# New tile order, split statistics and a rewritten instruction order at the start of the first MLP

## Chip, cores and metric

One core of a Trainium2 chip runs the whole chain. The metric is the time of one execution on the device in microseconds. The engines are TensorE (PE in the profile, its weight loads PEld), VectorE (DVE), ScalarE (ACT), GpSimd (POOL), and SyncE (SP), which starts most DMAs.

## The reference

Three layers follow one another; the output of each is the input of the next. B=4, H=8, S=768, D=40, so a batch is 768 tokens by 320 values: six tiles of 128 tokens, 24 tiles in all.

```python
# 1: linear attention over 768 steps, state 40x40 for each head
y[t] = r[t] @ state
Sa = state @ a[t]
state = state * w[t] - outer(Sa, b[t]) + outer(v[t], k[t])
# 2: Fourier mixing, then a channel MLP (320 -> 1280 -> 320)
u = x + real(fft(fft(x, axis=1), axis=2))
un = (u - mean(u)) / sqrt(var(u) + 1e-6)      # over the 320 channels of a token
x = u + relu(un @ w_ch1) @ w_ch2
# 3: token MLP (768 -> 256 -> 768), then a channel MLP (320 -> 1536 -> 320)
u = x + (relu(x.T @ w_tok1) @ w_tok2).T
out = u + relu(u @ w_ch1) @ w_ch2
```

## The kernel before

**Order.** Every instruction is first recorded by `Plan.op` with its engine and the buffers that it reads and writes. Nothing is scheduled by a rule: the string `ORDER` lists the numbers of the recorded operations in base 36, and `Plan.emit` issues them in that order. Each engine works through its own instructions in this order. A number followed by `:0` or `:1` names the PSUM banks that the operation takes, and `+12,y,0` puts twelve filler matmuls (`warm`, L54, on the identity) into a bank of the pool y.

**Attention.** Class `Attn` takes the sequence in 12 chunks of 64 steps; a small triangular inverse on VectorE, products on TensorE and selections on GpSimd follow each other in every chunk. Its result is X, the 24 tiles in SBUF; a batch's last tiles are written by the line X<-y (L434).

**Fourier mixing, batch by batch.** `fft` forms sums and differences of halves of X on VectorE (FP and FM L876, ef L877 and L878, sd L882, dd L888), splits each into a rounded part Xh and a rest Xl (L884, L885; Ds L889, L890), and multiplies with the transform tables in PSUM (psA, L900 and L915). The results are evacuated as a rounded part (ScalarE, L925) and a rest (VectorE, L926) into A. `fft2` then runs four mixing groups of eight matmuls "mix" (L947). Each is added to X while the sum over the channels is accumulated in sm (VectorE, L950), and a Square with accumulation gives ss (ScalarE, L953). Group 0 completes the tiles 0 and 3, group 1 the tiles 1 and 4, group 2 tile 2 and 96 rows of tile 5, and group 3 the other 32 rows of 5. After all six tiles one set of small instructions on 6 columns forms the variance v (L960), its square root y (ScalarE, L961), the reciprocal (L962), a Newton step (L963 to L966, four instructions) and the bias nb (L967).

**First channel MLP.** The tokens go through in six groups of four tiles, `tiles(g)`: tiles 0 to 3 of batch 0, then 4 and 5 of batch 0 with 0 and 1 of batch 1, and so on. `norm` applies y and nb (Y, L976 on VectorE, L978 on ScalarE), `turnp` transposes Y on TensorE (trp L1018) and evacuates it as cc, and `ch` multiplies: hps L1047, then acc L1037. The mixing of the next batch and the transposes of the next group are recorded within a group's `ch`.

**Token MLP and last MLP.** `tok` gives tps (L1179), `tok2` t2ps (L1192), which is added to X by X<-t2ps (L1194). `turnd` transposes the four tiles of a group with VectorE (L986, L987), stores and loads them again (dr_T, Z) and forms sums on GpSimd; `ch7` multiplies (sa and sb L1084, acc L1073).

**Decoding of weights.** Beside all this the weights, which lie in 64-bit numbers, are decoded in pieces: mdraw is loaded, mdt and mda are formed on VectorE (L853, L854, L856, L857), mdh on ScalarE (L855), and GpSimd finishes mda (L858, L859).

## Time and profile before

| | us |
|---|---|
| median of 3 runs | 979.46 |
| lowest and highest | 975.63, 984.27 |
| the profiled execution | 969.72 |
| its span, first to last instruction | 968.0 |
| TensorE busy | 914.7 (94%) |
| VectorE busy | 702.4 (73%) |
| ScalarE busy | 491.8 (51%) |
| GpSimd busy | 367.6 (38%) |
| warm fillers on TensorE, within its busy time | 74.2 |

The span is the time between the first and the last instruction of the profiled execution; its own time has 1.7 us more around it. Busy TensorE includes the fillers and the time in which a matmul runs at a low clock. The granted clock of the span was 0.974 of full speed. In the profile every fp32 matmul of the program is two records.

### The profile page before, as it was taken

Reading aid. Unit: us, or ns where it says so; the run is one execution under the profiler, and the core shown is the slowest. Engines: PE = TensorE matmul, PEld = TensorE weight load, DVE = VectorE, ACT = ScalarE, POOL = GpSimd, SP = SyncE. Lnnn points to the kernel's source line nnn. Section 1 sums busy time; section 2 is a strip of 40 time slices with the busy share of each in tenths; the row PEclk is TensorE's granted clock in tenths of the full one; section 3 lists DMA queues with packets and bytes.
Section 4 is the critical chain, followed back from the end, with each engine's and each line's share of the span. In section 5 each row is a group of like instructions: output and inputs, shape, how many; then the busy total and the mean of one; then the engine's idle time right before and its main releaser. Section 6 shows DMA issues by size and latency. Waiting matters only on the chain.

```text
span 968.0 us, 24200 instructions
## 1 busy us (share of the span) xinstructions
PE 914.7 (94%) x9657; PEld 848.1 (88%) x9657; DVE 702.4 (73%) x1527; ACT 491.8 (51%) x1068; POOL 367.6 (38%) x498
## 2 busy tenths in 40 slices
...
GB/s 213 155 169 174 174 196 215 180 199 203 170 183 171 180 242 286 287 140 194 126 172 123 151 86 109 132 166 374 144 175 86 80 50 79 101 1 99 1 28 28
...
## 3 DMA queue, kind: packets, MB, share of 16 engines
...
## 4 chain that ended last, share of the span: by engine, by line
PE 71%; DVE 9%; DMA 5%; ACT 3%; issue 2%; POOL 2%; SPq 1%; DVEq 0%; POOLq 0%; ACTq 0%
PE acc L1073 13%; PE hps L1047 9%; PE acc L1037 8%; PE sb L1084 7%; PE sa L1084 5%; PE sc L406 4%; PE kg L216 3%; PE warm L54 3%; PE tps L1179 2%; PE t2ps L1192 2%; PE y L428 1%; PE x L343 1%; PE s L367 1%; PE mix L947 1%; PE mg L291 1%
## 5 line engine op out<-in xcount | busy, mean ns | idle before, releaser
L1047 PE MATMUL hps<-cc,W1t 128*128 128x512 f32 x480 | 120.7, 395 | 0.0
L1037 PE MATMUL acc<-W,cc 128*128 128x320 f32 x720 | 116.1, 310 | 0.3 <-DMA W<-m11l 0.3
L1037 PEld LDWEIGHTS acc<-W,cc 128*128 128x128 f32 x720 | 109.0, 188 | 4.8 <-DMA W<-m11l 0.7
L1047 PEld LDWEIGHTS hps<-cc,W1t 128*128 128x128 f32 x480 | 87.9, 188 | 16.4
L1097 POOL TENSOR_TENSOR C<-C,C 128x256 f32<-128x256 f32 x36 | 27.4, 760 | 173.0 <-DVE W1t L1090 115.3
L1049 ACT ACTIVATE cc<-hps 128x512 fp32r<-128x512 f32 x60 | 35.8, 597 | 100.2 <-PE hps L1047 100.2
L1050 DVE SCALAR_TENSOR_TENSOR cc<-hps,cc 128x512 fp32r<-128x512 f32 x60 | 41.3, 688 | 56.6 <-ACT cc L1049 56.4
L54 PE MATMUL warm<-ident 128*128 128x128 f32 x454 | 74.2, 301 | 2.9 <-POOL ident masks.py:199 2.0
L216 PE MATMUL kg<-am,bt 120*128 120x192 f32 x242 | 55.7, 366 | 18.0 <-ACT am L136 15.7
L416 POOL TENSOR_SCALAR_AFFINE_SELECT sc<-sc 64x384 f32<-64x384 f32 (+1 forms) x72 | 42.3, 588 | 80.1 <-ACT sc L136 71.5
L225 POOL TENSOR_SCALAR_AFFINE_SELECT RT<-RT 64x384 f32<-64x384 f32 (+1 forms) x66 | 42.2, 659 | 78.4 <-ACT RT L136 77.2
L1091 DVE TENSOR_TENSOR C<-sb,C 128x256 f32<-128x256 f32 x108 | 44.2, 421 | 33.3 <-PE sb L1084 26.9
L54 PEld LDWEIGHTS warm<-ident 128*128 128x128 f32 x454 | 63.6, 207 | 5.2 <-POOL ident masks.py:199 2.0
L1073 PE MATMUL acc<-v,W1t 128*128 128x320 f32 x432 | 67.2, 309 | 0.0
L1073 PE MATMUL acc<-vb,W1t 128*128 128x320 f32 x432 | 66.9, 309 | 0.0
L1089 ACT ACTIVATE W1t<-C 128x256 fp32r<-128x256 f32 x108 | 41.9, 413 | 45.5 <-DVE C L1091 36.6
L1073 PEld LDWEIGHTS acc<-v,W1t 128*128 128x128 f32 x432 | 63.7, 188 | 0.1
L1073 PEld LDWEIGHTS acc<-vb,W1t 128*128 128x128 f32 x432 | 63.7, 188 | 0.0
L216 PEld LDWEIGHTS kg<-am,bt 120*128 120x128 f32 x242 | 43.0, 209 | 21.8 <-ACT am L136 16.8
L1090 DVE SCALAR_TENSOR_TENSOR W1t<-C,W1t 128x256 fp32r<-128x256 f32 x108 | 46.6, 450 | 19.4 <-ACT W1t L1089 19.0
L406 PE MATMUL sc<-rm,VZd 120*128 120x192 f32 x264 | 59.4, 358 | 0.3 <-ACT RT L136 0.3
L858 POOL TENSOR_TENSOR mda<-mda,mdh 128x320 f32<-128x320 f32 (+2 forms) x32 | 29.6, 933 | 72.2 <-ACT mdh L855 54.0
...
## 6 DMA issues: line engine op xcount, KB each, us to landing
...
mdraw<-in_moe_w_ch_dram SPq DMA_DIRECT2D x22, 320.0 KB
...
```

The lines of the kernel that those rows point to most:

```text
L54: for x in range(m): nc.tensor.matmul(t[:,128*(x%4):128*(x%4)+128],lhsT=ident,rhs=ident,start=True,stop=True)
L216: nc.tensor.matmul(ps[:,192*x:192*x+192],lhsT=bt[:,g+x].rearrange("p v t -> p (v t)"),rhs=am[:,:,g+x],start=True,stop=True)
L225: nc.gpsimd.affine_select(out=kv,in_=kv,pattern=[[0,3*m],[1,L]],compare_op=ALU.is_gt,fill=0.0,base=0,channel_multiplier=-1)
L406: for x,g in enumerate(gs): nc.tensor.matmul(ps[:,192*x:192*x+192],lhsT=VZd[:,g].rearrange("p v t -> p (v t)"),rhs=s.rm[:,:,g],start=True, ...
L416: nc.gpsimd.affine_select(out=o,in_=o,pattern=[[0,3*m],[-1 if rv else 1,L]],compare_op=ALU.is_gt,fill=0.0,base=L-1 if rv else 0,channel_mu ...
L1037: nc.tensor.matmul(s.pst(acc[x]),lhsT=a[:,sl],rhs=w2(w,m),start=(m==0 and n==0),stop=(m==MT-1 and n==2))
L1047: for n,(l,r) in enumerate(ops): nc.tensor.matmul(ps,lhsT=l,rhs=r,start=n==0,stop=n==7)
L1073: nc.tensor.matmul(s.pst(acc[x]),lhsT=a[:,sl],rhs=wv(w),start=(u==0 and y==0 and k==0),stop=(u==5 and y==1 and k==2))
L1084: for n,(y,x) in enumerate(((0,0),(0,1),(1,0),(2,2))): nc.tensor.matmul(R[r](),lhsT=va(q,y),rhs=S[:,x],start=first and n==0,stop=last and ...
L1089: s.act(256,lambda: nc.scalar.activation(out=Hh(y,c),in_=src(),func=AF.Relu),rd,[('Hh',z,y,c)],free=free)
L1090: s.dve(.33,lambda: V.scalar_tensor_tensor(out=Hl(y,c),in0=src(),scalar=0.0,in1=Hh(y,c).bitcast(F32),op0=ALU.max,op1=ALU.subtract),rd+[('H ...
L1091: def add(n,r,m,free): s.dve(.33,lambda: V.tensor_tensor(out=C(n),in0=R[r](),in1=C(m),op=ALU.add),[K[r],('C',m)],[('C',n)],free=free)
```

## The change

`TI=(0,3,1,4,2,5)` is a new order of a batch's six tiles. `tiles(g)` uses it, so that the first group takes the tiles 0, 3, 1 and 4 of batch 0, and the statistics sm, ss, v, y and nb hold their columns in this order. For batch 0 the root and its refinement are recorded in two sets, on the columns 0 to 3 and 4 to 5; for the other batches in one. The Newton step has three instructions in place of four: q=y*v, q=(q*-0.5)*y, y=(q+1.5)*y. `init` sets one value sq1 and takes its square root on ScalarE, which loads the table of the root there. The string `ORDER` is another one throughout. The lines of the new kernel stand one lower up to L953 and three or four lower behind it (v is L964, the reciprocal L966, Y L979 and L981, hps L1050).

```diff
+TI=(0,3,1,4,2,5)
...
     def init(s):
+        s.one(s.sq1,['sq1']); s.P.op('ACT',.1,lambda: s.nc.scalar.activation(out=s.sq1,in_=s.sq1,func=AF.Sqrt),[],['sq1'])
         s.zero(s.D1,['D1'],.63); s.one(s.D1[:,:,0:1],['D1'])
...
 ORDER="""
-0 1 5 4 2 fg 7 8 6 e 3 9 1b f g h +12,y,0 bx:0 1d 1f 1e a br 3s 1c 3u 8n 3v 3y 3w 7i 3t 7k 3x 3z j bk:1 by bz:0 bl i o m n k bm:1 bn b c d +3,y,0 s:0
...
-        Y=lambda: t["y"][b%2]; NB_=lambda: t["nb"][b%2]
-        s.dve(.07,lambda: V.tensor_scalar(out=t["v"],in0=t["ss"],scalar1=320.0**-3,scalar2=1e-6,op0=ALU.mult,op1=ALU.add),[('ss',i) for i in range(6)],['lv'])
-        s.act(54,lambda: nc.scalar.activation(out=Y(),in_=t["v"],func=AF.Sqrt),['lv'],[('ly',b%2)])
-        s.dve(.1,lambda: V.reciprocal(out=Y(),in_=Y()),[],[('ly',b%2)])
-        s.dve(.07,lambda: V.tensor_tensor(out=t["q"],in0=Y(),in1=Y(),op=ALU.mult),[('ly',b%2)],['lq'])
-        s.dve(.07,lambda: V.tensor_tensor(out=t["q"],in0=t["q"],in1=t["v"],op=ALU.mult),['lv'],['lq'])
-        s.dve(.07,lambda: V.tensor_scalar(out=t["q"],in0=t["q"],scalar1=-0.5,scalar2=1.5,op0=ALU.mult,op1=ALU.add),[],['lq'])
-        s.dve(.07,lambda: V.tensor_tensor(out=Y(),in0=Y(),in1=t["q"],op=ALU.mult),['lq'],[('ly',b%2)])
...
-    def tiles(s,g): return [divmod(4*g+x,6) for x in range(4)]
+        for c0,c1 in ((0,4),(4,6)) if b==0 else ((0,6),):
+            Y=lambda c0=c0,c1=c1: t["y"][b%2][:,c0:c1]; g=lambda n,c0=c0,c1=c1: t[n][:,c0:c1]; qs=TI[c0:c1]; z=c0//4
...
+            s.dve(.07,lambda g=g: V.tensor_scalar(out=g("v"),in0=g("ss"),scalar1=320.0**-3,scalar2=1e-6,op0=ALU.mult,op1=ALU.add),[('ss',i) for i in qs],kv)
+            s.act(54,lambda g=g,Y=Y: nc.scalar.activation(out=Y(),in_=g("v"),func=AF.Sqrt),kv,ky)
+            s.dve(.1,lambda Y=Y: V.reciprocal(out=Y(),in_=Y()),[],ky)
+            s.dve(.07,lambda g=g,Y=Y: V.tensor_tensor(out=g("q"),in0=Y(),in1=g("v"),op=ALU.mult),ky+kv,kq)
+            s.dve(.07,lambda g=g,Y=Y: V.scalar_tensor_tensor(out=g("q"),in0=g("q"),scalar=-0.5,in1=Y(),op0=ALU.mult,op1=ALU.mult),ky,kq)
+            s.dve(.07,lambda g=g,Y=Y: V.scalar_tensor_tensor(out=Y(),in0=g("q"),scalar=1.5,in1=Y(),op0=ALU.add,op1=ALU.mult),kq,ky)
...
+    def tiles(s,g): return [((4*g+x)//6,TI[(4*g+x)%6]) for x in range(4)]
```

What the new `ORDER` moves is seen in the engines' queues, at three places. The first is VectorE between the last X<-y of the attention and the first rest A of batch 0's transform (the first A<-psA,A in 128 rows). Before, two rows of FP and FM and two Xl stand between that product and this piece:

```order
L890 TENSOR_TENSOR Ds<-dd,Ds 32x161
L854 SCALAR_TENSOR_TENSOR mda_4959<-mdraw_4957,mdt_4958 128x320
L854 SCALAR_TENSOR_TENSOR mda_4951<-mdraw_4949,mdt_4950 128x320
L856 TENSOR_SCALAR mdt_4958<-mda_4959 128x320
L885 TENSOR_TENSOR Xl<-sd,Xh 128x353
L856 TENSOR_SCALAR mdt_4950<-mda_4951 128x320
L857 SCALAR_TENSOR_TENSOR mdt_4958<-mdraw_4957,mdt_4958 128x320
L877 TENSOR_TENSOR ef<-FP 128x3x161
L878 TENSOR_TENSOR ef<-FM 128x3x159
L888 TENSOR_TENSOR dd<-FM 32x161
L882 TENSOR_TENSOR sd<-ef 128x353
L926 TENSOR_TENSOR A_5461<-psA_5524,A_5460 128x208
```

And the same stretch of VectorE in the changed kernel, from FP to the first A in 128 rows; two Xl and a Ds stand ahead of the last X<-y:

```order
L877 TENSOR_TENSOR FP<-X 128x3x320
L854 TENSOR_SCALAR mdt_4907<-mdraw_4906 128x320
L855 SCALAR_TENSOR_TENSOR mda_4908<-mdraw_4906,mdt_4907 128x320
L854 TENSOR_SCALAR mdt_4915<-mdraw_4914 128x320
L886 TENSOR_TENSOR Xl<-sd,Xh 128x353
L927 TENSOR_TENSOR A_5468<-psA_5507,A_5468 64x208
L855 SCALAR_TENSOR_TENSOR mda_4916<-mdraw_4914,mdt_4915 128x320
L877 TENSOR_TENSOR FM<-X 128x3x320
L857 TENSOR_SCALAR mdt_4907<-mda_4908 128x320
L889 TENSOR_TENSOR dd<-FM 32x161
L879 TENSOR_TENSOR ef<-FM 128x3x159
L927 TENSOR_TENSOR A_5465<-psA_5524,A_5464 128x208
```

A, the smaller rest in 64 rows, is also new ahead of it; ef from FP, sd, the product of L857 and one of the L856 now stand behind.

The second place is the statistics of batch 0. VectorE before, from the variance v on:

```order
L960 TENSOR_SCALAR v<-ss 128x6
L853 TENSOR_SCALAR mdt_4950<-mdraw_4949 128x320
L856 TENSOR_SCALAR mdt_4954<-mda_4955 128x320
L962 RECIPROCAL y_5542<-y_5542 128x6
L854 SCALAR_TENSOR_TENSOR mda_4951<-mdraw_4949,mdt_4950 128x320
L963 TENSOR_TENSOR q<-y_5542 128x6
L926 TENSOR_TENSOR A_5463<-psA_5742,A_5462 128x208
L964 TENSOR_TENSOR q<-q,v 128x6
L926 TENSOR_TENSOR A_5464<-psA_5729,A_5464 64x208
L965 TENSOR_SCALAR q<-q 128x6
L857 SCALAR_TENSOR_TENSOR mdt_4954<-mdraw_4953,mdt_4954 128x320
L966 TENSOR_TENSOR y_5542<-y_5542,q 128x6
```

VectorE in the changed kernel, from the variance of four columns on:

```order
L964 TENSOR_SCALAR v<-ss 128x4
L927 TENSOR_TENSOR A_5468<-psA_5750,A_5468 64x208
L855 SCALAR_TENSOR_TENSOR mda_4908<-mdraw_4906,mdt_4907 128x320
L966 RECIPROCAL y_5563<-y_5563 128x4
L927 TENSOR_TENSOR A_5468<-psA_5750,A_5468 64x208
L964 TENSOR_SCALAR v<-ss 128x2
L967 TENSOR_TENSOR q<-y_5563,v 128x4
L968 SCALAR_TENSOR_TENSOR q<-q,y_5563 128x4
L889 TENSOR_TENSOR dd<-FM 32x161
L969 SCALAR_TENSOR_TENSOR y_5563<-q,y_5563 128x4
L927 TENSOR_TENSOR A_5467<-psA_5732,A_5466 128x208
L970 SCALAR_TENSOR_TENSOR nb_5561<-sm,y_5563 128x4
```

One multiplication and four decode rows fewer stand there, and a second v for two columns is among them. ScalarE at the same place before, squares and root:

```order
L889 ACTIVATE Ds<-dd 32x161
L953 ACTIVATE sq,ss<-X,sm 128x320 x6
L961 ACT_TABLE_LOAD
L961 ACTIVATE y_5542<-v 128x6
L925 ACTIVATE A_5462<-psA_5742 128x208
L855 ACTIVATE mdh_4956<-mda_4955 128x320
L925 ACTIVATE A_5464<-psA_5729 64x208 x2
```

ScalarE in the changed kernel, where the table load stands ten rows ahead of this, between two A of the same transform:

```order
L856 ACTIVATE mdh_4909<-mda_4908 128x320
L954 ACTIVATE sq,ss<-X,sm 128x320 x5
L926 ACTIVATE A_5468<-psA_5750 64x208
L954 ACTIVATE sq,ss<-X,sm 128x320
L965 ACTIVATE y_5563<-v 128x4
L926 ACTIVATE A_5468<-psA_5750 64x208
L926 ACTIVATE A_5466<-psA_5732 128x208
```

Six squares stand ahead of the first root in both; an A is now among them.

The third place is VectorE at the end of the first batch's token MLP, where X<-t2ps completes tiles and the transposes for the last MLP follow (acc there is the last part of the MLP before). Before, the last piece is:

```order
L1182 SCALAR_TENSOR_TENSOR cc<-tps,cc 128x320
L1194 TENSOR_TENSOR X<-t2ps,X 128x320
L987 STREAM_TRANSPOSE Y<-X 128x4x32
L986 STREAM_TRANSPOSE Y<-X 128x2x4x32
L987 STREAM_TRANSPOSE Y<-X 128x4x32
L1194 TENSOR_TENSOR X<-t2ps,X 128x320
L987 STREAM_TRANSPOSE Y<-X 128x4x32 x2
L986 STREAM_TRANSPOSE Y<-X 128x2x4x32
```

In the changed kernel:

```order
L1185 SCALAR_TENSOR_TENSOR cc<-tps,cc 128x320
L1197 TENSOR_TENSOR X<-t2ps,X 128x320
L989 STREAM_TRANSPOSE Y<-X 128x2x4x32
L990 STREAM_TRANSPOSE Y<-X 128x4x32 x2
L1197 TENSOR_TENSOR X<-t2ps,X 128x320
L990 STREAM_TRANSPOSE Y<-X 128x4x32 x2
L989 STREAM_TRANSPOSE Y<-X 128x2x4x32
L1197 TENSOR_TENSOR X<-t2ps,X 128x320
L989 STREAM_TRANSPOSE Y<-X 128x2x4x32
L990 STREAM_TRANSPOSE Y<-X 128x4x32 x2
```

The last transposes stand behind the fifth X<-t2ps of the batch now, behind the fourth before. TensorE in this stage has 12 fillers in the order, 4 before; in the whole kernel there are 238, 227 before.

## Rows read from the trace of the kernel before

**Rows 1.** Stages of the span: busy us (and instructions) of each engine, granted clock, DMA.

```profile
0.00:340.00 340.00, 300.09 (x5091) 268.51 (x5092) 275.14 (x520) 245.60 (x453) 139.44 (x217) 0.94 0.85 185
...
384.10:400.30 16.20, 12.87 (x90) 11.56 (x90) 14.99 (x30) 5.37 (x16) 5.34 (x7) 0.83 0.74 244
...
400.30:419.20 18.90, 18.67 (x142) 17.16 (x141) 15.60 (x50) 11.44 (x29) 7.48 (x10) 0.96 0.68 241
...
419.20:671.50 252.30, 249.60 (x1445) 224.03 (x1444) 172.77 (x366) 94.92 (x209) 117.66 (x127) 1.00 0.52 158
...
671.50:723.40 51.90, 50.63 (x342) 48.63 (x341) 37.40 (x96) 16.56 (x42) 19.98 (x26) 1.00 0.53 167
...
723.40:968.00 244.60, 241.11 (x1829) 240.44 (x1827) 160.85 (x419) 92.53 (x266) 56.19 (x75) 1.00 0.18 59
```

**Rows 2.** Timeline of 383 to 402 us: start, length, engine, line, [idle before].

```profile
384.92 1.16 DVE L876 TENSOR_TENSOR FP<-X 128x960 f32<-128x960 f32 x1
...
394.08 1.18 DVE L926 TENSOR_TENSOR A<-psA,A 128x208 fp32r<-128x208 f32 x3
...
394.51 0.48 PE L900 MATMUL psA<-T,Xh 128*128 128x208 f32 x2 [2.06 <-DVE A L926]
...
400.33 1.90 PE L947 MATMUL mix<-T,A 128*128 128x322 f32 x7
```

**Rows 3.** Groups of VectorE, 384.9 to 419.1 us: busy, mean ns | idle before.

```profile
L926 DVE TENSOR_TENSOR A<-psA,A 128x208 fp32r<-128x208 f32 (+1 forms) x12 | 4.4, 373 | 1.1 <-ACT A L925 0.8
...
L950 DVE SCALAR_TENSOR_TENSOR X<-mix,X 128x320 f32<-128x320 f32 (+2 forms) x7 | 3.2, 488 | 2.4 <-PE mix L947 2.4
...
L857 DVE SCALAR_TENSOR_TENSOR mdt<-mdraw,mdt 128x320 f32<-128x320 uint16 x3 | 2.1, 716 | 0.0
...
L885 DVE TENSOR_TENSOR Xl<-sd,Xh 128x353 fp32r<-128x353 f32 x4 | 2.1, 520 | 0.0
...
L856 DVE TENSOR_SCALAR mdt<-mda 128x320 int32<-128x320 int32 x4 | 2.0, 490 | 0.0
...
L877 DVE TENSOR_TENSOR ef<-FP 128x483 f32<-128x483 f32 x2 | 1.3, 650 | 0.0
...
L853 DVE TENSOR_SCALAR mdt<-mdraw 128x320 int32<-128x320 int32 x3 | 1.0, 319 | 0.0
```

**Rows 4.** Timeline of 402 to 420 us.

```profile
408.28 1.28 ACT L961 ACT_TABLE_LOAD   x1
...
408.63 0.17 DVE L960 TENSOR_SCALAR v<-ss 128x6 f32<-128x6 f32 x1
...
409.81 0.19 DVE L962 RECIPROCAL y<-y 128x6 f32<-128x6 f32 x1 [0.54 <-ACT y L961]
...
413.86 0.72 DVE L976 TENSOR_SCALAR Y<-X,y,nb 128x256 f32<-128x256 f32 x2
```

**Rows 5.** Line L964 over the span (min/median/max ns), then timeline of 564 to 569.5 us.

```profile
L964 DVE TENSOR_TENSOR q<-q,v x4: 558/962/1030, 410.8 to 566.6; 128x6 f32<-128x6 f32 x4
...
564.62 0.89 DVE L960 TENSOR_SCALAR v<-ss 128x6 f32<-128x6 f32 x1
...
566.54 1.02 POOL L820 TENSOR_TENSOR mdt<-mda,mda 128x384 f32<-128x384 f32 x1
...
566.60 0.98 DVE L964 TENSOR_TENSOR q<-q,v 128x6 f32<-128x6 f32 x1
```

**Rows 6.** Timeline of TensorE, 695 to 710 us.

```profile
705.27 0.39 PE L54 MATMUL warm<-ident 128*128 128x128 f32 x2
...
705.41 1.13 PE L1192 MATMUL t2ps<-W1t,k 128*128 128x320 f32 x6
```

**Rows 7.** Timeline of TensorE, 345 to 358 us, then two stretches by engine and clock.

```profile
350.09 0.20 PE L367 MATMUL s<-VZt,kbt 128*40 128x40 f32 x1 [1.96 <-issue]
...
350.00:358.00 8.00, 7.91 (x65) 7.05 (x64) 3.62 (x8) 1.67 (x4) 2.59 (x5) 0.57 1.05 287
...
394.50:400.30 5.80, 4.93 (x23) 4.68 (x24) 4.87 (x11) 2.90 (x8) 2.02 (x2) 0.53 0.47 142
```

More of the change, by code (lines that the diff above doesn't have):

```diff
@@ L664 @@
+3hq 3i1 3in 3i3 3ij 3hl 3if 3i4 3i7 3id 3ie 3ho 3ig 3ia 3j5:10 3j6 3j9 3ja 3ik 3io 3it 3iq 3iu 3ip 3ib 3ic 3i8 3i9 3j3 3j4 3jb 3ir 3is 3iy 3j7 3iv
+3jt:01 3ju 3jx 3j8 3jc 3jh 3ji 3je 3jy 3iw 3ix 3jr 3jv 3iz 3j0 3j1 3j2 3js 3jd 3jz 3jj 3jm 3jw 3k2 3k0 3k5 3k6 3jn 3jf 3jg 3jk 3jl 3kf 3jp 3jq 3k1 3k7
+3kd 3ke 3jo 3kg 3ka 3kb 3kc 3k8 3k9 3k3 3k4 3ki 3kj 3kh 3kk 3kn 3ko 3kp 3kq 3kl 3km 3kr 3ks
 """
```

266 lines of the change are left out of this document (133 added, 133 removed).

## Prediction

> **What bounds the kernel now.** I read the times first: the profiled execution took 969.72 us, of which the span is 968.0, so it lies 9.7 below the median of the three timed runs (979.46). All sums below are made against 969.72 and then moved up by 9.7. Next I cut the span into stages [rows 1]. From 419.20 on TensorE is busy 249.60 of 252.30 us, then 50.63 of 51.90, then 241.11 of 244.60: there only its amount of work counts. The first 340 us, the attention, keep it busy for 300.09, with DVE at 275.14 beside it. The changed code is at its loosest between 384.10 and 419.20, the junction from the attention to the first channel MLP. In 384.10 to 400.30 TensorE works for 12.87 of 16.20 us and DVE for 14.99; in 400.30 to 419.20 TensorE looks busy (18.67 of 18.90), but much of that is the filler matmuls "warm", which stand in the order while it has nothing else. So before 400.3 DVE's queue sets the pace, and after it a chain: four mixing groups, squares, root, small DVE rows, normalisation, transposes, first "hps".
>
> **Junction A, last attention product to first mixing matmul.** The first difference of the last attention rows starts at 384.92, the first rest A of the transform at 394.08, 9.16 us later, and TensorE's psA matmuls waited 2.06 us for it; the mixing starts at 400.33 [rows 2]. The first fence of the order lists what stands between. Gone from there are two Xl (0.52 each), the small Ds (0.32 at most, as short as the shortest decode row), one L856 (0.49), one L857 (0.72), the sum ef from FP (0.65) and one sd (0.52, by the Xl of the same width): 3.7 us [rows 3]. New are two L853 (0.32 each) and one A (0.37): 1.0. Net -2.7. Two Xl and the Ds now stand ahead of the last X<-y product, which two L853 have left: 1.36 - 0.64 = +0.7. That ef and sd return behind the first A, against which one A has gone ahead: +0.8, which I cost at nothing, since DVE there waited 0.8 for ScalarE's evacuation [rows 3]; without that cover it is +0.8. **A = -2.0**. Bounds: if the 2.06 us of PE wait and some of what follows at a low clock go too, -5; if only what is added counts, +1.5.
>
> **Junction B, mixing to first "hps", 18.9 us.** Three pieces. (1) The stretch from v to the first Y on DVE is 408.63 to 413.86, 5.23 us; in it DVE stood idle 0.54 for the root, which sat behind a table load of 1.28 [rows 4]. With the load moved forward that idle goes. The second fence shows what else leaves: L853 0.32, L856 0.49, L857 0.72, ef 0.65, one A 0.37 [rows 3], and one multiplication, which took 0.56 here [rows 5]: with the idle 3.65. New there are a second v (0.17) and dd (0.32): net -3.1. (2) The decode rows went somewhere: ahead of v there are now two more L856 and two more L857 (the new lines are one higher), 2.4 us. DVE waited 2.4 us for the mixing matmuls [rows 3], mostly ahead of the first X<-mix; there the new order puts an L856, an Xl and the Ds, 0.49 + 0.52 + 0.32 = 1.3, of which the last two stood behind it before. That much is covered: +1.1. (3) Behind the first Y the second statistics set puts five small rows (0.17 to 0.23) and the A that left, against the ef that left: 0.9 + 0.37 - 0.65 = +0.6. **B = -1.4.** Bounds -3.1 (all of 2 and 3 covered) to +1.9 (of 1 only the 0.54 and the 0.56 are gained, 2 costs 2.4 and 3 costs 0.6).
>
> The tiling by itself would allow more: tiles 0, 3, 1 and 4 are ready after two of the four mixing groups. But the new order, by its rows, does not take it. ScalarE still does five squares, one A and the sixth square before the four-column root (second pair of fences), and TensorE still runs all four mixing groups and the next batch's transform ahead of the first "hps". So I count nothing for it.
>
> **Token stage, 671.5 to 723.4.** Fillers in the program go from 4 to 12 there. One is two rows in the trace, and a pair pushes the following matmul by 0.14 us (705.27 to 705.41) [rows 6]; the records overlap, but each of two records costs 0.14 at full pipelining at most, so 16 rows cost up to 2.2. TensorE's idle is 1.27 in this stage [rows 1], and the fillers stand where it would wait: 2.2 - 1.2 = **+1.0**. The third fence shows a second thing: the last transposes of the tiles for the final MLP now come after the fifth X<-t2ps, not the fourth. One such group takes TensorE 1.13 [rows 6]. The work that hides it is that of three other batches, some 39 us of matmuls between 684 and 723; uncovered it costs 1.1. Bounds 0 to +3.3.
>
> **Everything else.** In the attention, DVE and ScalarE rows are reshuffled. Counting by the order what stands ahead of each of the 12 chunks' last state rows, priced by the group means, gives differences of -1.9 to +3.1 us, the last four of them 0.0. DVE has slack of 65 us there [rows 1]. I take 0 and keep both ends. The new memset and the root on one column (ScalarE, 0.2 like any small row) lie beside TensorE's work. For batches 1 to 3 the refinement is one short row fewer, beside a full TensorE: 0. The channel and final MLPs have the same matmuls: 0.
>
> Sum: -2.0 - 1.4 + 1.0 = -2.4, so 967.3 in an execution like the profiled one, and **977.1** as a median.
>
> **Rivals.** *R1, the low clock goes, faster.* TensorE stalled 1.96 us at 348.1 to 350.1, where no wait is shown, and afterwards ran at a mean clock of 0.57 for 8 us; after the 2.06 us wait for A it ran at 0.53 for 5.8 us [rows 2, 7]. These means lie near 1.2 GHz, the lower of its two levels. At 2.4 GHz the 7.91 busy us would be shorter by 43%, 3.4, and the 4.93 by 47%, 2.3. If the shorter queue at A keeps the clock up and the stall does not recur, that is 1.96 + 3.4 + 2.3 = 7.7 more: 979.5 - 2.4 - 7.7 = 969.4. For: the wait at A gets shorter by A's own sum. Against: by that sum it only just vanishes, and the change does nothing to the stall at 348.
>
> *R2, small rows held behind GpSimd, slower.* The multiplication L964, 6 columns wide, took 558 to 1030 ns, and at 564.62 even v took 0.89 where the same row took 0.17 at 408.63; at 566.54 a GpSimd row of 1.02 ran beside the one of 0.98 [rows 4, 5]. So a small row that meets a GpSimd row costs about 0.8 more. Before, 7 such rows stand on the path from squares to normalisation of batch 0, one of them held by 0.4. Now there are 12 in two sets. All held: 12 x 0.8 - 0.4 = +9.2, and 979.5 - 2.4 + 9.2 = 986.3; the change loses from the fourth held row on, at 0.8 each against 2.4 of gain and the 0.4 of before. For: GpSimd is busy 7.48 of 18.90 us in that stage [rows 1]. Against: before, one of seven was held, and by that rate the 12 would hold two. The Trainium skill, "SBUF — State Buffer", section "Who interferes with whom", says that DVE and GpSimd share one pair of ports as an exclusive lock, and that a DVE instruction with two SBUF inputs, as each step of the new refinement is, contends with a GpSimd instruction that reads SBUF, the loser waiting for the whole of it. The trace agrees as far as it goes (0.98 beside 1.02), so a shorter refinement made only of such rows is no sure gain.
>
> *R3, the change does not do what it says.* The order keeps squares and mixing ahead, the chain at the junction gets no shorter (A and B 0), and the fillers cost their 2.2: 981.7. For: the fences. Against: the rows that left DVE's queue at A are plain.
>
> **How the numbers follow.** About 1%, 9.8 us, is what a measurement of this kernel can tell from no change; its three runs lie 0.9% apart. Forecast (977.1, its own bounds about 971 to 984) 0.56; R1 (969.4) 0.18; R2 (986.3) 0.13; R3 (981.7) 0.13. Faster by over 1% means under 969.7: rather over half of R1 and a little of the forecast's spread, 0.15. Slower by over 1% means over 989.3: half of R2, and the upper attention end together with the uncovered token cost, 0.10. Within 1%: 0.75. The range 967 to 988 takes in the forecast with its bounds, R3, R1 and R2 when most rows are held; what is left outside is R1 with a further gain in the attention, and R2 together with a loss there.
>
> **What the changed profile would show.** Right: the table load among the A evacuations, before the squares, and no idle of DVE ahead of the reciprocal; the first A some 2 us nearer to the FP row; root rows of 4 and of 2 columns, the first only after six squares; mixing start to first "hps" still 18 to 19 us; token stage about 53. Wrong: the first "hps" before the third or fourth mixing group's squares (then the tiling pays, by several us); small rows of 0.9 among the two sets (R2); a clock near 1.0 in 394 to 400 and 350 to 358 (R1); a chunk of the attention that ends several us earlier or later, which none of my terms would explain.

## The result and the profile after

| | median us | ratio to before, 95% interval |
|---|---|---|
| changed kernel, 20 runs | 977.73 (970.58 to 987.95) | 1.0074 [1.0048, 1.0099] |
| kernel before, 20 runs beside it | 975.54 (962.58 to 987.62) | |
| changed kernel again: a0, a1, a2 | 981.84, 978.85, 980.54 | 1.0118, 1.0074, 1.0099 |
| kernel before against itself: b0 | 969.36 | 0.9995 [0.9956, 1.0034] |

The ratio compares the executions of each kernel that lie within 1.5% of its fastest, which leaves out 8 of 20 of the kernel before and 1 of 20 of the changed one; over all 20 the medians differ by 0.22%. The repeats put the cost at 0.7 to 1.2%. The forecast was a gain of 2.4 us, from 979.46 to 977.1. That 977.1 lies close to the measured 977.73 is luck: it was counted from the median of three runs of the kernel before that all lie above the median of its twenty (975.54). The profiled execution of the changed kernel took 974.34 us (span 972.6).

The stages of the changed kernel, busy time of PE, PEld, DVE, ACT and POOL, then clock and DMA; they answer to [rows 1]:

```profile
0.00:340.00 340.00, 298.04 (x4959) 266.37 (x4961) 273.77 (x513) 241.25 (x444) 132.93 (x214) 0.93 0.85 181
388.70:402.90 14.20, 10.25 (x76) 9.39 (x73) 13.78 (x28) 6.45 (x15) 5.00 (x6) 0.84 0.54 165
402.90:423.00 20.10, 19.48 (x147) 18.16 (x146) 17.50 (x55) 9.91 (x28) 7.29 (x11) 0.94 0.83 293
423.00:673.70 250.70, 248.75 (x1445) 224.16 (x1444) 173.62 (x365) 95.15 (x211) 121.31 (x128) 1.00 0.51 158
673.70:727.60 53.90, 52.56 (x358) 50.62 (x357) 37.62 (x96) 16.51 (x42) 20.25 (x26) 1.00 0.56 179
727.60:972.60 245.00, 241.11 (x1829) 240.58 (x1828) 160.81 (x419) 92.49 (x267) 55.80 (x75) 1.00 0.17 57
```

In these two profiles the junction is 2.0 shorter up to the mixing and 1.2 longer behind it, the channel MLP 1.6 shorter, the token stage 2.0 longer, the last stage 0.4 longer. All this begins 4.6 us later: FP stands at 389.49, not 384.92. The start of the junction, to be read beside [rows 2] and [rows 3] (timeline; start, length, idle before in brackets):

```profile
389.49 1.16 DVE L877 TENSOR_TENSOR FP<-X 128x960 f32<-128x960 f32 x1
...
393.92 1.28 ACT L143 ACT_TABLE_LOAD   x1
...
395.26 1.19 DVE L927 TENSOR_TENSOR A<-psA,A 128x208 fp32r<-128x208 f32 x3
395.68 0.47 PE L901 MATMUL psA<-T,Xh 128*128 128x208 f32 x2 [0.59 <-DVE A L927]
396.36 1.34 DVE L878 TENSOR_TENSOR ef<-FP 128x483 f32<-128x483 f32 x1
397.62 1.15 DVE L858 SCALAR_TENSOR_TENSOR mdt<-mdraw,mdt 128x320 f32<-128x320 uint16 x1
398.69 0.95 DVE L883 TENSOR_TENSOR sd<-ef 128x353 f32<-128x353 f32 x2
399.56 0.64 DVE L927 TENSOR_TENSOR A<-psA,A 128x208 fp32r<-128x208 f32 x2
400.35 2.90 PE L54 MATMUL warm<-ident 128*128 128x128 f32 x12 [2.96 <-DVE A L927]
402.91 0.61 PE L948 MATMUL mix<-T,A 128*128 128x322 f32 x1
```

The first A comes 5.77 us behind FP, where it was 9.16. But ef, an L858 and two sd now stand between the first A and the last two, and TensorE waits 2.96 for those, ahead of its fillers and the mixing. The wait for the first A fell from 2.06 to 0.59. At the place of the 2.96 the kernel before waits 0.86 (timeline):

```profile
398.18 2.50 PE L54 MATMUL warm<-ident 128*128 128x128 f32 x10 [0.86 <-DVE A L926]
```

The statistics, to be read beside [rows 4], from the same timeline:

```profile
412.84 0.16 DVE L964 TENSOR_SCALAR v<-ss 128x4 f32<-128x4 f32 x1
...
413.11 0.35 ACT L926 ACTIVATE A<-psA 64x208 fp32r<-64x208 f32 x1 [2.51 <-PE psA L916]
413.36 0.54 ACT L954 ACTIVATE sq<-X,sm 128x320 bf16<-128x320 f32 x1
413.50 0.37 DVE L927 TENSOR_TENSOR A<-psA,A 64x208 fp32r<-64x208 f32 x1 [0.49 <-ACT A L926]
413.90 0.20 ACT L965 ACTIVATE y<-v 128x4 f32<-128x4 f32 x1
414.31 0.17 DVE L966 RECIPROCAL y<-y 128x4 f32<-128x4 f32 x1
416.41 1.25 DVE L979 TENSOR_SCALAR Y<-X,y,nb 128x256 f32<-128x256 f32 x4
```

The table load is out of the way and VectorE does not idle for the root, as forecast. All small rows of both sets take 0.15 to 0.17 on VectorE. The low clock at 350 to 358 [rows 7] is gone (1.00), but it is gone from the repeat of the kernel before too (b0, 1.00), so this is not the change's doing. The one ahead of the mixing stayed (0.84 in 388.70 to 402.90).

### The profile page after: what moved, and what is told of

It reads as the page before. It is cut to its first block, busy times and chain, and to the rows that moved or that the text cites. A ratio compares the mean times of both kernels' runs of the same rounds, so it can differ in the third digit from the quotient of the medians.

```text
span 972.6 us, 24245 instructions
## 1 busy us (share of the span) xinstructions
PE 915.8 (94%) x9679; PEld 850.3 (87%) x9679; DVE 706.6 (73%) x1529; ACT 493.4 (51%) x1070; POOL 367.5 (38%) x499
## 4 chain that ended last, share of the span: by engine, by line
PE 73%; DVE 9%; DMA 7%; ACT 3%; SPq 3%; issue 1%; POOL 0%; DVEq 0%; ACTq 0%
PE acc L1076 13%; PE hps L1050 11%; PE acc L1040 10%; PE sb L1087 7%; PE sa L1087 5%; PE kg L217 3%; PE sc L407 3%; PE warm L54 3%; SPq L134 2%; PE tps L1182 2%; PE t2ps L1195 2%; PE mix L948 2%; DMA Mst<-Md 1%; DVE pr L250 1%; PE x L344 1%
## 5 line engine op out<-in xcount | busy, mean ns | idle before, releaser
L1050 PE MATMUL hps<-cc,W1t 128*128 128x512 f32 x480 | 121.0, 396 | 0.0
L1050 PEld LDWEIGHTS hps<-cc,W1t 128*128 128x128 f32 x480 | 87.8, 188 | 16.6 <-DVE cc L1053 0.2
L54 PE MATMUL warm<-ident 128*128 128x128 f32 x476 | 79.0, 305 | 5.0 <-DVE A L927 3.0
L54 PEld LDWEIGHTS warm<-ident 128*128 128x128 f32 x476 | 68.9, 212 | 7.3 <-ACT Xh L885 3.1
L226 POOL TENSOR_SCALAR_AFFINE_SELECT RT<-RT 64x384 f32<-64x384 f32 (+1 forms) x66 | 40.1, 625 | 82.0 <-ACT RT L136 79.2
L1093 DVE SCALAR_TENSOR_TENSOR W1t<-C,W1t 128x256 fp32r<-128x256 f32 x108 | 47.2, 454 | 20.2 <-ACT W1t L1092 19.7
L217 PEld LDWEIGHTS kg<-am,bt 120*128 120x128 f32 x242 | 43.2, 209 | 19.7 <-ACT am L136 16.0
L407 PE MATMUL sc<-rm,VZd 120*128 120x192 f32 x264 | 56.6, 343 | 2.1 <-DMA VZd<-in_vR_dram 1.9
L859 POOL TENSOR_TENSOR mda<-mda,mdh 128x320 f32<-128x320 f32 (+2 forms) x32 | 30.6, 959 | 58.1 <-ACT mdh L856 34.9
```

The costliest lines, as they stand in the source:

```text
L54: for x in range(m): nc.tensor.matmul(t[:,128*(x%4):128*(x%4)+128],lhsT=ident,rhs=ident,start=True,stop=True)
L217: nc.tensor.matmul(ps[:,192*x:192*x+192],lhsT=bt[:,g+x].rearrange("p v t -> p (v t)"),rhs=am[:,:,g+x],start=True,stop=True)
L407: for x,g in enumerate(gs): nc.tensor.matmul(ps[:,192*x:192*x+192],lhsT=VZd[:,g].rearrange("p v t -> p (v t)"),rhs=s.rm[:,:,g],start=True, ...
L1050: for n,(l,r) in enumerate(ops): nc.tensor.matmul(ps,lhsT=l,rhs=r,start=n==0,stop=n==7)
L1093: s.dve(.33,lambda: V.scalar_tensor_tensor(out=Hl(y,c),in0=src(),scalar=0.0,in1=Hh(y,c).bitcast(F32),op0=ALU.max,op1=ALU.subtract),rd+[('H ...
```

## The experiments

All order experiments sort a part of `ORDER` by the order of the other kernel, with its filler entries and banks; each diff shows the first entries that differ. "To hps" is the time of the first hps. Pieces, in us:

| kernel | FP | FP to mix | mix to hps | hps to tps | tps to sb | ratio |
|---|---|---|---|---|---|---|
| before | 384.9 | 15.4 | 18.9 | 252.2 | 46.9 | |
| b0 before again | 395.0 | 14.3 | 19.7 | 251.6 | 47.0 | 0.9995 [0.9956, 1.0034] |
| after | 389.5 | 13.4 | 20.1 | 250.6 | 48.9 | 1.0074 |
| a0, a1, a2 (after again) | 399.1, 398.2, 395.8 | 12.8, 13.5, 12.7 | 20.5, 20.5, 20.2 | 250.6 | 48.6 to 49.0 | 1.0118, 1.0074, 1.0099 |
| e1 after, attention as before | 385.1 | 14.7 | 20.2 | 250.6 | 48.9 | 1.0037 [1.0000, 1.0075] |
| e2 before, attention as after | 395.8 | 13.5 | 19.9 | 251.5 | 47.0 | 1.0066 [1.0028, 1.0105] |
| e3 after, no token fillers | 395.1 | 12.7 | 20.5 | 251.8 | 48.4 | 1.0101 [1.0060, 1.0141] |
| e5 after, one decode job later | 390.5 | 12.4 | 20.6 | 252.5 | 48.7 | 1.0062 [1.0024, 1.0099] |
| e6 after, first part as before | 393.3 | 13.3 | 19.7 | 250.6 | 49.0 | 1.0048 [1.0014, 1.0081] |
| e12 after, second part as before | 393.4 | 14.1 | 20.3 | 250.5 | 48.7 | 1.0043 [1.0004, 1.0082] |
| e7 e1 without fillers ahead of mix | 378.2 | 9.0 | 25.7 | 251.3 | 48.8 | 1.0013 [0.9980, 1.0046] |
| e8 e1 with the token stage as before | 389.4 | 14.8 | 20.7 | 250.5 | 47.1 | 1.0001 [0.9966, 1.0036] |
| e9 before, one load later | 388.5 | 14.2 | 19.8 | 250.8 | 47.1 | 0.9988 [0.9955, 1.0022] |
| e10 e8 with early statistics | 389.6 | 14.7 | 16.6 | 257.7 | 47.0 | 1.0014 [0.9975, 1.0053] |
| e13 after, decode rows as before | 395.9 | 13.0 | 20.3 | 250.6 | 48.8 | 1.0128 [1.0073, 1.0183] |
| e14 before, decode rows as after | 388.1 | 14.6 | 19.7 | 251.7 | 47.3 | 1.0060 [1.0027, 1.0093] |
| e15 after, GpSimd rows cut | 399.3 | 12.4 | 20.4 | 250.6 | 48.9 | one run, 983.58 |
| e16 e8, last rows of the attention as after | 392.4 | 12.4 | 20.6 | 250.6 | 47.1 | 1.0049 [1.0011, 1.0086] |

**The attention against the rest (a0, e1, e2).** e1 and e2 exchange the first 2231 (2224) entries, which reach up to the FP row.

```diff
-4 2 9 a fi 8 g 3 b 1d h i
+4 2 fi 9 a 8 g 3 b 1d h i
```

> The changed kernel once more, as the base for the others of this call. Theory 1 (the new order of the attention is slower): the difference of the last attention rows (FP) starts again some 4 us later than before's 384.9, near 389, and the median is 2 to 7 us above before's. Theory 2 (the 4.6 us of the attention were chance of one execution): FP starts anywhere from 383 to 390, and the median lies within 2 us of before's. Both: from FP to the first mixing matmul about 13.4, from there to the first hps about 20.

> The changed kernel with the attention's operations (all that stands up to the last attention products, 12 chunks with the loads, decode rows and fillers among them) put back into the order of before; junction, MLPs and token stage stay new. Theory 1 (the attention's order costs 4 to 5 us): 4 to 5 us below the changed kernel on the median, FP near 385. Theory 2 (chance): within 2 us of the changed kernel, FP not earlier than there. Theory 3 (the loss is made at the junction and by the token fillers, B +2.6 and token +1 against the forecast): within 2 us of the changed kernel as well, first mix to first hps about 20, token stage about 53.

> The reverse: the kernel of before with the attention's operations in the new order, everything from the junction on as before, and without the early table load. Theory 1: 4 to 5 us slower than before, FP near 389. Theory 2: within 2 us of before. Theory 3: within 2 us of before, since junction and token stage are before's.

With the old attention the changed kernel falls to 1.0037, where the unaltered one beside it has 1.0118; with the new attention the kernel before rises to 1.0066. So the larger part of the loss sits ahead of FP. What differs there is seen by cutting the time to the first hps into TensorE's idle time, what the low clock takes from its busy time (busy x (1 - granted clock), summed over windows of 20 us), and the rest:

| | old attention: before, e1, e7, e8, e9 | new: after, a0, a1, a2, e2, e3, e15 |
|---|---|---|
| to hps | 412.9 to 424.9, mean 419.9 | 423.0 to 432.4, mean 429.4 |
| TensorE idle | 40.8 to 48.4, mean 44.2 | 46.7 to 52.6, mean 49.0 |
| low clock | 16.1 to 28.1, mean 21.0 | 19.2 to 30.0, mean 24.7 |
| rest | mean 354.8 | mean 355.6 |
| VectorE waits for DMA | 28.5 to 33.0, mean 30.0 | 36.3 to 43.6, mean 40.2 |
| idle in 60 to 100 us | mean 7.9 | mean 9.9 |
| idle from 240 us to 25 us ahead of mix | 3.6 to 6.2, mean 4.9 | 5.8 to 10.8, mean 8.8 |

The work is the same; idle time is 4.8 longer, and VectorE stands 10 us longer in front of transfers. Two kernels with the old attention are not in the table: b0, with its first hps at 429.0, 45.8 idle and 26.6 of waits, and e10, which has 11 fillers less than e8, with 420.9, 49.6 and 29.9. The 2.0 in 60 to 100 us are a shift: over the first 80 us TensorE idles 30.2 in the old order and 29.7 in the new.

VectorE's longer waits for transfers are no measure of the loss. Its waits for TensorE's products sc (L412 of the changed kernel) fall from a mean of 15.3 to 8.3 in the same profiles (up to 25 us ahead of the mixing). And e12, e14 and e16 wait 30.8, 32.3 and 29.6 for transfers, as the old order does, and still take 1.0043 to 1.0060.

Single profiles do not separate the low clock of the two orders, but the granted clock of every execution is on record. Its means, over the executions that the ratios compare:

| | granted clock | kernel before beside it |
|---|---|---|
| whole attention old: e1, e7, e8, e9, e10, b0 | 0.9725, 0.9747, 0.9720, 0.9723, 0.9740, 0.9741 | 0.9718 to 0.9736 |
| whole attention new: a0, a1, a2, e2, e3 | 0.9658, 0.9683, 0.9683, 0.9652, 0.9665 | 0.9728 to 0.9736 |
| parts of it exchanged: e5, e6, e12, e13, e14, e16 | 0.9715, 0.9712, 0.9694, 0.9638, 0.9688, 0.9712 | 0.9728 to 0.9760 |

The whole new attention runs at a clock lower by 0.005 to 0.008. Among the 141 such executions of the kernel before, 0.001 of clock goes with 0.74 us. By this, as an estimate, 3 to 6 of the 7 to 11 us that a0, a1, a2, e2 and e3 are slower in the mean go with the lower clock. The rest does not: e5 and e6 are within 0.002 of the clock beside them and still at 1.0062 and 1.0048. (The first series of the changed kernel has 0.9692; none is on record beside it.)

VectorE's waits for DMA from 240 us to 25 us ahead of the mixing (total, times, longest) of the kernel before are one line:

```profile
DVE dt L494 <- DMA draw<-in_moe_w_ch_dram: 6.0, 1, 6.0
```

and of the changed kernel's repeat a0:

```profile
DVE dt L495 <- DMA draw<-in_moe_w_ch_dram: 8.9, 2, 6.0
DVE mdt L854 <- DMA mdraw<-in_moe_w_ch_dram: 5.5, 1, 5.5
DVE Mt L252 <- DMA N<-Gd: 2.8, 2, 2.4
DVE da L496 <- DMA m10l<-da: 2.3, 1, 2.3
```

One of these can be followed to TensorE in the timeline of a0. An L854 waits for its mdraw, ys stands behind it in VectorE's queue, and a product waits for ys:

```profile
368.48 0.33 DVE L854 TENSOR_SCALAR mdt<-mdraw 128x320 int32<-128x320 int32 x1 [5.48 <-DMA mdraw<-in_moe_w_ch_dram]
...
373.36 0.67 PE L425 MATMUL y<-Sbd,r 120*64 120x120 f32 x4 [4.50 <-DVE ys L442]
```

Behind this wait TensorE runs at the lower of its two clocks for 10 us (windows; the granted clock is the third number from the end):

```profile
373.40:383.40 10.00, 10.00 (x123) 9.20 (x125) 7.93 (x14) 6.03 (x11) 6.47 (x8) 0.50 0.71 170
```

In `after` the same pair waits 1.79 and 0.82, in e3 6.23 and 5.25, in e2 4.54 and 3.57. But in a1 and a2 it waits only 1.14 and 0.4, and 1.63 and 0.7, and these two profiled executions (983.33 and 980.12) are about as long as that of a0 (983.47).

**Which rows of the attention (e5, e6, e9, e12, e13, e14, e16).** e5 moves the decode job of that L854 (four VectorE rows, one on ScalarE, a store and the next load) behind the ys; e9 puts its load, in the kernel before, behind the four loads that follow it; e6 and e12 sort only the first 1497 entries (to about 270 us) or only the others back; e13 and e14 exchange the places of the decode operations alone.

e5, against the changed kernel:

```diff
-1nc 1iy 1j0 1jd:0 1nd 1ne 1nj 1m8 1nf
+1iy 1j0 1jd:0 1m8 1ja:1
...
+1nc 1nd 1ne 1nj 1nf 1ng 1o5
```

e9, against the kernel before:

```diff
-1n9 1ip:1 1iq 1jq 1jr 1j2:1 1j3
+1ip:1 1iq 1jq 1jr 1j2:1 1j3
...
+1n9
```

e6 begins as e1. e12, e13 (against the changed kernel) and e14 (against the one before) begin:

```diff
-11v 11x 121 5p 179 175 14i:0
+11v 175 14f:0 5p 11x 179 145
...
-3r 3s 3t
+3r 44 45 3s 3t
...
-3r 3p 42 43 mt
+3r 3p mt
```

> The changed kernel with one decode job moved: its four rows on VectorE (the first of which waits for its load mdraw near the end of the attention), its row on ScalarE, its store and the next load now stand behind the row ys of the tenth chunk, ahead of which they stood. Theory 1a (that row holds VectorE for 1.8 to 6.2 us, and TensorE then waits up to 5.3 for ys): the wait of TensorE for ys near 370 us shrinks to under 1 us, and the time from the last LT rows (354 us) to FP falls from 38 to 43 us to about 37; the median is 3 to 5 us below the changed kernel's 1.0118 of before. Rival 1b (the load itself is late, whoever waits for it): the same wait turns up in a later row, and the median moves under 1.5 us.

> The changed kernel with only the first part of the attention in the order of before (the first 1497 operations, up to about 270 us), the rest as changed. Theory 1a (the late decode row is the larger part of the loss): about a third of what the whole attention gave back, 2 to 4 us below the changed kernel, and the wait for ys of 3.6 to 5.3 us is still there. Rival 1c (the loss is spread over the first chunks: the later key rows at 100 us, the waits for Mst and AT): two thirds or more, 5 to 8 us below.

> The kernel of before with one load moved: the load mdraw of the first decode job near the end of the attention now stands behind the four other loads that follow it on SyncE's queue, so that it is issued some 3.5 us later (352 in place of 348.8); the decode row on VectorE keeps its place at 358.7. Theory 1a (a decode row that meets its load late holds VectorE, and with it sc, ys and TensorE): the row waits 2 to 6 us, TensorE waits for ys near 365 to 370, FP starts 2 to 5 us later than before's 384.9 and the median is 2 to 5 us above before's. Rival 1b (VectorE has slack there and catches up, or the load lands in time anyway): no wait of TensorE over 1 us for ys, and the median within 1.5 us of before's.

> The changed kernel a third time, as the base for this call, since its first two series gave 1.0074 and 1.0118 of before. All theories: FP between 389 and 399 us, VectorE waits some 40 us for DMAs ahead of 400 us (28 to 31 in the kernels with the old order of the attention), median 1.006 to 1.012 of before.

> The changed kernel with only the second part of the attention (operations 1497 to 2231, from about 270 us on) in the order of before; the counterpart of the kernel with only the first part. Theory 1a (the late decode row there is the larger part): 4 to 6 us below the changed kernel, and no wait for ys over 1 us near 370. Theory 1c (the loss is spread over the first chunks): 2 to 3 us below, FP near 391.

> The changed kernel, its attention's operations in the new order, but every operation of the weight decoding (loads, VectorE, ScalarE and GpSimd rows, stores) put back to where before has it, counted in operations of the attention ahead of it. Theory 1 in its narrow form (it is the decode rows that hold VectorE for their loads and stores): 5 to 8 us below the changed kernel, VectorE's waits for DMAs near 30 us, FP near 386. Rival 1d (it is the order of the attention's own rows, its loads and inversions): within 2 us of the changed kernel.

> The reverse: the kernel of before with every operation of the weight decoding ahead of the junction put where the changed kernel has it, and nothing else. Theory 1 in its narrow form: 5 to 8 us above before, VectorE's waits for DMAs near 40 us. Rival 1d: within 2 us of before, waits near 30.

In e9 the row waited 1.57 and TensorE not at all, so a wait of this length cost nothing there; one as long as the 5.48 of a0 was not tried in the old order. e5 takes the one wait away (no wait for ys near 370) and brings 1.0062, within the error of the changed kernel. Either half put back brings 1.0043 to 1.0048, as near to the kernel before as both halves together (e1, 1.0037), so the runs do not show how the loss divides. The decode rows of the new order do harm in the old attention (e14, 1.0060; VectorE waits 4.4 there for a store of mda, and TensorE's idle from 240 us is 9.0), but the decode rows of the old order do not mend the new attention (e13, 1.0128). It looks as if the places of decode rows and of attention rows fit each other in either order; that was not tested further. My narrow theory, the one job, fell.

> The changed kernel with its first 2197 order entries (all of the attention up to the last rows of the last chunk) in the order of before and everything from the token MLP on in the order of before; the end of the attention, the junction and the first channel MLP stay as changed. Theory: this keeps the one gain that was shown, 2 us from FP to the first mixing matmul, and takes neither the attention's loss nor the 0.5 of the token stage, so FP comes at 379 to 389, FP to mix at 13 to 13.5, mixing to hps at 20 to 20.5, and the ratio to before is 0.996 to 1.000. Rival: the loss sits in the order's last rows of the attention or behind it; then FP comes late (393 or more) and the ratio stays at 1.004 or more.

```diff
-1mk 1lt:1 1mh 1mj 1lu 1lv 1lw 1lq:0
+1mh 1mk 1mj 1lt:0 1lq:1 1lr 1lu 1lv
```

e16 differs from e8 in the last 34 entries ahead of FP, which stay as changed. It should have kept the gain of junction A; FP came at 392.4 and the ratio is 1.0049, against 1.0001 of e8, with intervals that overlap. By its expectation the rival is the nearer. Whether the last rows cost something is left open.

**The comparison itself (b0, a2).**

> The kernel before, unchanged, timed like all the others against the kernel before. Theory (the changed order really costs some 0.7 per cent): this gives 1.000 with an interval that holds 1, the last differences between kernels of 0.002 and less are noise, and its profile has TensorE idle for 41 to 48 us and 16 to 28 us lost to the low clock ahead of the first hps, as in the five profiles with the attention in the order of before. Rival: the comparison itself, which leaves out the runs far above the fastest of each kernel, pushes any kernel with fewer runs up; then this too gives 1.004 or more.

> The changed kernel, unchanged, in the same call. Theory: 1.005 to 1.012, with 46 to 53 us of TensorE idle time ahead of the first hps, VectorE waiting for DMA for 38 to 44 us there, and the pieces from FP to mixing 12.5 to 13.5 and from mixing to hps 20 to 20.5 us. Rival (most of the 0.7 per cent is the comparison or chance): within 0.003 of the kernel before in this call.

The kernel before against itself gives 0.9995, so the method does not make the 0.7 to 1.2%. The profiled execution of b0 (979.26, above its median of 969.36) had TensorE idle for 45.8 us ahead of the first hps, as the others of that order, but 26.2 at the low clock and FP at 394.98: one profile's FP time says little.

**The token stage (e3, e8).**

e3 against the changed kernel (eight such entries), and e8 against e1, where everything from the token MLP on is sorted:

```diff
-+3,acc,0
...
-+1,acc,0
...
-2ep 2f4 2f2 2ex 2f1 2ev
+2ep 2er 2f2 2f1 2ez 2ex
```

> The changed kernel without the 12 fillers of the token stage (4 of which stood there before too). Theory 3 (the stage's 2 us more are these fillers): first tps to first sb 2 to 3 us shorter than in the changed kernel, and the median lower by as much. Rival (the fillers stand where TensorE waits anyway, and the 2 us come from the later transposes): the stage keeps its length within 0.5 us and idle time of TensorE appears in the fillers' places.

> The changed kernel with the attention in the order of before and also everything from the token MLP on; the second product of the token MLP goes through the tiles in the new order 0 3 1 4 2 5, so that the transposes of the first group again stand behind the fourth X<-t2ps. Theory 3b (the 1.9 us of the token stage are in its order, not in its fillers): first tps to first sb 46.9 to 47.2 in place of 48.9, and the median about 2 us below the kernel with only the attention put back, which brings it to the level of before or 1 us below. Rival (the new tile order makes the stage longer by itself): it stays at 48.5 or more.

First tps to first sb, in e3 and then in e8 (windows):

```profile
680.10:728.50 48.40, 45.80 (x297) 43.32 (x296) 32.80 (x82) 14.92 (x37) 17.27 (x21) 1.00 0.51 163
```

```profile
675.40:722.50 47.10, 45.99 (x306) 44.25 (x305) 32.78 (x81) 14.71 (x37) 17.21 (x21) 1.00 0.53 167
```

Without its 12 fillers the new stage takes 48.4, not 48.9 (48.6 to 49.0 in the repeats): TensorE is then idle for 2.6 instead of busy. With the old order, and 4 fillers, it takes 47.1 and idles 1.1. So the order costs about 1.4 and the fillers 0.5 at most.

**The junction (e7, e10, e15).**

e7 against e1, then e10 against e8:

```diff
-24h 1q4 +6,acc,0 22r:0
+24h 1q4 22r:0
...
-232 233 291 234 24u:1 24v 1pu
+232 238 239 24u:1 233 234 23a 23b 23c
```

e15 against the changed kernel:

```diff
-j=n%3; due=rel+40
+j=n%3; due=rel+40; w=8 if nm=="w2" and n in (5,6) else d
...
-nc.gpsimd.tensor_tensor(out=g("da").bitcast(F32),in0=g("da").bitcast(F32),in1=g("dh").bitcast(F32),op=ALU.subtract)
+nc.gpsimd.tensor_tensor(out=g("da")[:,:w].bitcast(F32),in0=g("da")[:,:w].bitcast(F32),in1=g("dh")[:,:w].bitcast(F32),op=ALU.subtract)
```

> The changed kernel with the attention in the order of before and without the six fillers (12 rows) that stand right ahead of the first mixing matmul. Theory 4 (they run at the low clock after A is there, and hold the mixing up): from FP to the first mix 14.7 falls to 12.0 to 12.8 us, and of these 2 to 2.7 us all arrive at the first hps. Rival (they only fill a wait, or the mixing then runs longer at the low clock): FP to first hps stays within 0.7 us of the 34.9 of the kernel with them.

> The changed kernel with attention and token stage in the order of before, and with the order at the junction written so that it takes what the tiles 0 3 1 4 allow: variance, root (ahead of the fifth and sixth square on ScalarE), refinement and Y of the four tiles directly behind their squares on VectorE, the transposes behind the transform's small part, the first hps ahead of the rest of the next batch's transform; the decode rows, FP and A rows that stood between come later, 18 fillers less. Theory 5 (the changed order left the gain of the tiling lying): first mix to first hps 13 to 16 us in place of 20.2 to 20.7, and 2 to 5 us of that remain at the end, 2 to 5 below before. Rival (the rows that were passed are needed soon after: the weights of the second product, the next batch's mixing): the stretch is shorter, but from hps to the token stage it is longer by as much, and the median is within 1.5 us of the kernel without it, 1.0001 of before.

> The changed kernel, in which the four GpSimd rows that finish mda for two weight pieces (the ones that run between the last rows of the first transform and the statistics) work on 8 columns of 320; these weights stay unfinished. Theory: the term for the stretch from the first mixing matmul to the first hps was wrong because these GpSimd rows, of 0.87 to 1.74 us, run beside VectorE's two Xl (1.19 and 1.49 us against 0.52 [rows 3]), an L858 (0.97 against 0.49) and FP (1.44 against 1.16), which makes 2.3 us of held rows against 0.4 before; in seven more runs of this order at this place the same rows were held by 2.0 to 2.5. Then all of these fall to their plain lengths, the 0.65 wait for the store of mda goes, and mixing to first hps comes down from 20.1 to 20.5 us to 18.3 to 18.9, or 18.8 if the Xl lie under the wait for the mixing. Rival: the rows are long for another reason (what they read, the placing of their buffers) or their length is covered; then they stay as they are, or the stage stays at 20 or more.

e7: without these six fillers (12 rows) FP to hps is 34.7, against 34.9 in e1. In these profiles they cost nothing; the wait moves from ahead of the mixing to behind it.

e10 takes what the tiling offers: statistics and Y of the four tiles directly behind their squares (11 fillers less than e8). The first hps comes 16.6 us after the mixing starts instead of 20.7, but hps to tps grows from 250.5 to 257.7. Its timeline behind the first hps shows TensorE waiting for work of batch 1 that was pushed back:

```profile
424.53 0.47 PE L901 MATMUL psA<-T,Xh 128*128 128x208 f32 x2 [0.85 <-DVE A L927]
426.01 0.57 PE L948 MATMUL mix<-T,A 128*128 128x322 f32 x2 [0.45 <-ACT A L926]
...
429.10 3.63 PE L1050 MATMUL hps<-cc,W1t 128*128 128x512 f32 x8 [1.09 <-DVE X L951]
```

In this profile four us are gained and seven given back; the ratios of e10 and e8 differ by less than their error.

e15 asks why the stretch behind the mixing is long. In the changed kernel VectorE rows run slow beside GpSimd rows (timeline):

```profile
401.51 1.74 POOL L859 TENSOR_TENSOR mda<-mda,mdh 128x320 f32<-128x320 f32 x1 [2.04 <-ACT mdh L856]
402.44 2.61 DVE L886 TENSOR_TENSOR Xl<-sd,Xh 128x353 fp32r<-128x353 f32 x2
...
406.98 0.49 DVE L855 SCALAR_TENSOR_TENSOR mda<-mdraw,mdt 128x320 int32<-128x320 int32 x1 [0.65 <-DMA m11l<-mda]
...
407.93 0.89 POOL L859 TENSOR_TENSOR mda<-mda,mdh 128x320 f32<-128x320 f32 x1
408.21 0.97 DVE L858 SCALAR_TENSOR_TENSOR mdt<-mdraw,mdt 128x320 f32<-128x320 uint16 x1
409.78 1.44 DVE L877 TENSOR_TENSOR FP<-X 128x960 f32<-128x960 f32 x1
```

The same stretch in e15, where those GpSimd rows have 8 columns:

```profile
411.33 1.08 POOL L859 TENSOR_TENSOR mda<-mda,mdh 128x8 f32<-128x8 f32 x1 [2.04 <-ACT mdh L856]
412.26 0.97 DVE L886 TENSOR_TENSOR Xl<-sd,Xh 128x353 fp32r<-128x353 f32 x2
...
416.72 0.49 DVE L855 SCALAR_TENSOR_TENSOR mda<-mdraw,mdt 128x320 int32<-128x320 int32 x1 [1.57 <-DMA m11l<-mda]
417.68 0.22 POOL L859 TENSOR_TENSOR mda<-mda,mdh 128x8 f32<-128x8 f32 x1
417.95 0.49 DVE L858 SCALAR_TENSOR_TENSOR mdt<-mdraw,mdt 128x320 f32<-128x320 uint16 x1
419.00 1.16 DVE L877 TENSOR_TENSOR FP<-X 128x960 f32<-128x960 f32 x1
```

The four VectorE rows (two Xl, the L858, FP) fall to their plain lengths, so the GpSimd rows did hold them, by 2.4 us. The Trainium skill, "SBUF — State Buffer", section "Who interferes with whom", says that VectorE and GpSimd share ports as an exclusive lock; these rows agree. Yet in the one execution of e15 mixing to first hps stays 20.4: VectorE now waits 1.57 for the store of mda, where it waited 0.65, and 0.77 for the mixing. This is what the rival of that expectation said: the held rows are covered, mostly by a decode row that waits for a DMA ahead of the third X<-mix. From FP to hps e15 takes 32.8, the four profiles of the changed kernel 32.9 to 34.0.

## Why the prediction was wrong

**Attention, forecast 0 with ends -1.9 and +3.1: the step that failed.** "Counting by the order what stands ahead of each of the 12 chunks' last state rows, priced by the group means" adds up lengths of rows. It puts at nothing what the new places do to TensorE's waits and to its clock, and no rival had more of either. The last X<-y of 64x360, which both orders have ahead of the junction, comes 3.9 later in the two profiles, outside the ends:

```profile
378.99 0.53 DVE L434 TENSOR_TENSOR X<-y,PT 64x360 f32<-64x360 f32 x1 [0.34 <-PE y L428]
```

```profile
382.88 0.53 DVE L435 TENSOR_TENSOR X<-y,PT 64x360 f32<-64x360 f32 x1 [0.33 <-PE y L429]
```

One profile says little of this, as b0 shows (389.06 for the same row of the kernel before). What shows it are the exchanges: the new attention alone costs the kernel before 0.66%, some 6 us (e2), and without it the changed kernel is at 1.0037 (e1). In place of the 0 the runs showed the same work with some 5 us more idle time of TensorE up to the first hps and a clock lower by 0.005 to 0.008. "DVE has slack of 65 us there" was true as a sum and no protection. Which rows make TensorE wait is not shown: one decode row that waits for its load can be followed to TensorE (a0), but taking this wait away did not clearly gain time (e5).

**A, forecast -2.0, measured -1.3 in the two profiles; near in size, not in working.** From FP to the mixing 2.0 are gone, but FP itself stands 0.7 later behind that X<-y, as the forecast has it in its sum. The first A gained 3.4. The part "ef and sd return behind the first A, against which one A has gone ahead: +0.8, which I cost at nothing" failed: with the L858 they stand ahead of the last A, two of them run at 1.34 and 1.15 (0.65 and 0.49 elsewhere), and TensorE waits 2.96 there, where it waited 0.86.

**B, forecast -1.4, measured +1.2: wrong sign, within its bounds.** Ahead of v +1.6 (forecast +1.1), with the wait for the store among it, which I had not seen coming. From v to the first Y -1.7 (forecast -3.1): the idle time at the root went, but VectorE idles 0.49 for an A, small rows that depend on each other take 0.19 each where I priced 0.17 and less, and the L856 and L857 that left had taken 0.32 and 0.48 there, not their group means of 0.49 and 0.72. Behind the first Y +1.3 (forecast +0.6). Part of the +1.2 is the one profile of before: its 18.9 is 19.7 to 19.8 in b0, e9 and e14, which have the same junction, so the repeats put B nearer +0.8.

**A and B together.** Counted from that X<-y, the first hps comes 40.2, 40.0, 40.7 and 40.2 later in before, b0, e9 and e14, and 40.1, 39.9, 40.6 and 39.5 later in after, a0, a1 and a2. The means are 40.3 and 40.0: the junction gained 0.2 to 0.3, less than profiles of one kernel differ by, and not 3.4.

**Token stage, forecast +1.0, measured +2.0.** Within bounds; but about three quarters come from the order, which I had costed at nothing because other batches' matmuls would hide it, and a quarter at most from the fillers, on which the term rested.

**Channel MLP, forecast 0, measured -1.6** in the two profiles. Over the other kernels, e10 apart, it takes 250.5 to 252.5 with either order; not followed up.

**Rivals.** R1: the stall at 348 went, the low clock did not; with the new attention there is more of it. R2 at the place that it named (the small rows) did not occur; its mechanism took other rows, and in the one execution of e15 their release gained nothing. R3 was nearest: A and B together are close to 0, the token stage costs 2, and the tiling's offer was not taken; the profile of e10 shows it given back when taken alone. R3 too had the attention at 0.

**Open.** Which rows ahead of FP make up the loss is not settled, nor why the clock is lower with them; the one job that was moved is not the whole of it. None of the kernels beats the one before by more than the error (e9 0.9988, e8 1.0001).
